# Written order on every engine, weights in 32 pieces, one buffer for each order of v

## The chip, the cores and the metric

The kernel runs on one core of a Trainium2 chip. The metric is the device time of one execution in microseconds (us); lower is better. Every time of a run is a median of several executions, taken on the same chip in the same rounds as the kernel before; readings of a trace are those of one profiled execution. Runs of different rounds stood on different chips: a difference between two such runs is good to some 2 us, and the ratios to before are the safer comparison.

## The reference, cut to what matters

A gated linear attention feeds a two-layer MLP with a quick GELU.

```python
# q, k, v, f_logit: (4, 8, 768, 48) float32
f = 1 / (1 + np.exp(-f_logit))
for t in range(S):
    state = f[:, :, t, :, None] * state + np.einsum('bhd,bhe->bhde', k[:, :, t], v[:, :, t])
    y[:, :, t] = np.einsum('bhd,bhde->bhe', q[:, :, t], state)
x = y.transpose(0, 2, 1, 3).reshape(3072, 384)
h = x @ w_in                                  # (384, 2048)
out = (h * (1 / (1 + np.exp(-1.702 * h)))) @ w_out   # (2048, 384)
```

The weights arrive as 64-bit floats, and the kernel builds 32-bit floats from their two halves.

## The kernel before

The 3,072 tokens are cut into twelve units of 256. For each unit the attention runs as a ladder of steps (six score levels, two transposes of k, the state, the output y). y is copied to yT and moved by DMA into xT, and the MLP matmuls h (on xT and w_in) and o (on g and w_out) follow. The program is written so that MLP matmuls of earlier units stand between the attention steps of the current one, as `fill`.

Only TensorE runs in the order in which the program is written. The framework's scheduler orders all other engines:

```python
ctx.enter_context(tc.manual_schedule(engines={mybir.EngineType.PE}))
```

The transposes by which VectorE brings the loads of f, q and k into place are called turns. A piece of a weight is converted by one ScalarE and six VectorE operations, in a chain:

```python
nc.scalar.activation(a, hi.bitcast(F32), AF.Abs, scale=2.0 ** 112)
ve.tensor_scalar(si, hi, -(1 << 31), -(1 << 31), op0=ALU.bitwise_and, op1=ALU.bitwise_xor)
ve.tensor_scalar(a, a, 2.0 ** 97, None, op0=ALU.max)
ve.scalar_tensor_tensor(si, ai, 3, si, op0=ALU.logical_shift_left, op1=ALU.bitwise_xor)
ve.tensor_scalar(ai, si, -(1 << 23), None, op0=ALU.bitwise_and)
ve.scalar_tensor_tensor(a, lo.bitcast(U32), 2.0 ** -52, a, op0=ALU.mult, op1=ALU.mult)
ve.tensor_tensor(dst, a, s, ALU.add)
```

There are 28 pieces (12 of 512 columns, 16 of 384), converted during units 0 to 2. One buffer holds all orders in which a unit's v is read, and it is loaded after the whole of the last unit:

```python
vl = ld.tile([P, NV, DM], F32, tag="vl", name=f"vl_{n}")      # pool ld has bufs=1
...
            if n + 1 < NALL:
                load(n + 1)          # at the end of a unit's attention
```

One queue, SyncE's, issues every load, every store and the moves from yT to xT.

## Time and profile before

| | before |
|---|---|
| median of 3 (lowest to highest) | 758.95 us (757.6 to 759.25) |
| profiled span | 761.1 us |
| TensorE matmul, busy | 676.3 us (89%) |
| VectorE, busy | 415.4 us (55%) |
| ScalarE, busy | 188.2 us (25%) |
| moved by DMA | 76.4 MB |

The 55% of VectorE is an average of two stages. In the first 200 us it does the conversion besides the attention; after that it is half idle and TensorE binds. The lines that show this stand in the prediction: the row of slices (each digit is the busy tenths of one fortieth of the span), a table of stretches, waits, and a few marks of the timeline.

### The profile page before, as it was taken

The page shows a single profiled execution, that of the slowest core. Times are in us where ns is not written, and L with a number is a line of the kernel's source. Part 1 is how long each engine was busy: PE and PEld are TensorE (multiplying, and loading weights), DVE is VectorE, ACT ScalarE, POOL GpSimd, SP SyncE. Part 2 cuts the span into 40 slices and gives each one's busy share as a digit, 9 for nine tenths or more (in the row PEclk, how much of TensorE's full clock was granted, in tenths as well). Part 3 has the DMA queues.
Part 4 walks back from the last instruction along what each step waited for, and adds up shares of the span by engine and source line. Part 5 has one row for each costly group of instructions (what it writes and reads, how often), then busy time and mean ns, then how long its engine had stood idle before and what let it go on. Part 6 is the DMA issues. An engine that isn't in the chain of part 4 may idle for free.

```text
span 761.1 us, 20034 instructions
## 1 busy us (share of the span) xinstructions
PE 676.3 (89%) x8864; PEld 499.3 (66%) x8864; DVE 415.4 (55%) x679; ACT 188.2 (25%) x365; POOL 38.5 (5%) x80
## 2 busy tenths in 40 slices
PE   0551577879999999999999999999999999999998
PEld 0440355656768768768668678678677687687684
DVE  6779659789565555455455555456445545352020
ACT  1132123132222222222223223222222222132120
POOL 2010002000100100100100100100100001000000
PEclk9955687989999999999999999999999999999999
DMA  9955775857461351441550550550542402100100
GB/s 200 226 122 136 167 158 140 198 151 155 114 134 52 101 136 43 121 119 39 135 134 10 145 135 1 148 130 28 155 98 65 102 12 86 42 13 7 37 0 21
DMA packets 78182, 76.40 MB, mean 100 GB/s; under 512 B 31504, under 2 KB 72976, under 8 KB 78096
## 3 DMA queue, kind: packets, MB, share of 16 engines
q1 hardware_dynamic: 78096, 75.13, 40.6%
q8 instruction: 69, 1.13, 0.7%
q14 instruction: 17, 0.14, 0.1%
HBM read 65.67 MB, written 9.44 MB: 99 GB/s over the span
## 4 chain that ended last, share of the span: by engine, by line
PE 79%; DVE 9%; DMA 6%; SPq 2%; issue 2%; POOL 0%; ACT 0%; DVEq 0%; POOLq 0%; ACTq 0%
PE h L452 32%; PE o L468 31%; PE sc L251 6%; PE y L304 5%; DMA raw<-in_q_dram 2%; DMA bits<-in_moe_w_out_dram 2%; PE sc L378 1%; PE tkn L362 1%; DVE X L290 1%; DMA bits<-in_moe_w_in_dram 1%; PE y L412 1%; DVE a L165 1%; DVE s L162 1%; DMA v_tok<-in_v_dram 1%; DVE A L275 1%
## 5 line engine op out<-in xcount | busy, mean ns | idle before, releaser
L452 PE MATMUL h<-xT,w_in 128*128 128x256 f32 x1152 | 271.8, 388 | 20.2 <-DMA xT<-yT 20.2
L468 PE MATMUL o<-w_out,g 128*128 128x384 f32 x768 | 267.4, 499 | 5.9 <-DVE g L458 5.9
L452 PEld LDWEIGHTS h<-xT,w_in 128*128 128x128 f32 x1152 | 216.7, 193 | 55.4 <-issue 21.5
L468 PEld LDWEIGHTS o<-w_out,g 128*128 128x128 f32 x768 | 144.3, 193 | 101.6 <-DVE g L458 7.7
L458 DVE TENSOR_TENSOR g<-h,sg 128x256 f32<-128x256 f32 x192 | 81.0, 423 | 167.8 <-ACT sg L457 167.8
L457 ACT ACTIVATE sg<-h 128x256 f32<-128x256 f32 x192 | 73.6, 384 | 176.8 <-PE h L452 176.7
L290 DVE TENSOR_TENSOR X<-X,tot 128x1024 f32<-128x1024 f32 x60 | 73.1, 1218 | 37.6 <-PE sc L251 37.6
L294 ACT COPY Kc<-X 128x512 f32<-128x512 f32 x60 | 37.7, 628 | 185.5 <-DVE X L290 185.5
L304 PE MATMUL y<-A,vl 64*48 64x64 f32 (+1 forms) x2688 | 63.4, 237 | 13.8 <-issue 8.4
L304 PEld LDWEIGHTS y<-A,vl 64*48 64x48 f32 x2688 | 52.9, 126 | 18.9 <-issue 12.6
L275 DVE TENSOR_TENSOR A<-sc,masks 128x512 f32<-128x512 f32 (+1 forms) x84 | 62.6, 755 | 0.0
L219 DVE STREAM_TRANSPOSE X<-raw 128x1024 f32<-128x1024 f32 x24 | 49.2, 2051 | 16.0 <-PE sc L251 11.9
L251 PEld LDWEIGHTS sc<-X,Kc 48*64 48x64 f32 x1920 | 35.6, 141 | 24.6 <-issue 13.4
L251 PE MATMUL sc<-X 48*64 48x128 f32 (+1 forms) x768 | 25.4, 274 | 29.6 <-DVE X L219 26.3
L251 PE MATMUL sc<-X,Kc 48*64 48x64 f32 x1920 | 43.3, 230 | 6.3 <-DVE A L275 5.4
L251 PEld LDWEIGHTS sc<-X 48*64 48x64 f32 x768 | 20.3, 149 | 42.0 <-issue 20.2
L234 POOL TENSOR_TENSOR tot<-F 128x512 f32<-128x512 f32 x12 | 12.8, 1065 | 601.7 <-DVE st L393 592.9
L420 ACT COPY yT<-y 48x1024 f32<-48x1024 f32 x24 | 24.2, 1008 | 56.5 <-PE y L412 50.9
L290 DVE TENSOR_TENSOR X<-X,F 128x1024 f32<-128x1024 f32 x12 | 14.7, 1226 | 38.7 <-PE sc L251 38.7
L159 ACT ACTIVATE a<-bits 128x384 f32<-128x384 f32 (+1 forms) x28 | 16.8, 609 | 48.5 <-DVE w_out L166 22.2
L219 DVE STREAM_TRANSPOSE F<-raw 128x1024 f32<-128x1024 f32 x12 | 24.3, 2025 | 4.6 <-DMA raw<-in_f_logit_dram 4.6
L242 DVE TENSOR_TENSOR X<-X,F 128x1024 f32<-128x1024 f32 x12 | 15.4, 1286 | 17.6 <-PE y L412 17.6
(35 smaller groups left out, 274.0 us busy)
## 6 DMA issues: line engine op xcount, KB each, us to landing
vl<-v_tok SPq DMA_DIRECT2D x60, 192.0 KB
bits<-in_moe_w_out_dram SPq DMA_DIRECT2D x16, 384.0 KB
raw<-in_f_logit_dram SPq DMA_DIRECT2D x24, 192.0 KB
bits<-in_moe_w_in_dram SPq DMA_DIRECT2D x12, 384.0 KB
raw<-in_q_dram SPq DMA_DIRECT2D x24, 192.0 KB
raw<-in_k_dram SPq DMA_DIRECT2D x24, 192.0 KB
v_tok<-in_v_dram SPq DMA_DIRECT2D x12, 384.0 KB
vl<-v_tok SPq DMA_DIRECT2D x12, 384.0 KB
```

The lines of the kernel that those rows point to most:

```text
L159: nc.scalar.activation(a, hi.bitcast(F32), AF.Abs, scale=2.0 ** 112)
L219: nc.vector.transpose(out.rearrange("p (a i j) -> p a j i", a=NP, j=R), raw[:, j].rearrange("p a (j d) -> p (a j) d", j=R)[:, :, :32],)
L251: nc.tensor.matmul(out[g * HS:(g + 1) * HS, h, a, :], lhsT=lhs(h, a * U + g * G), rhs=rhs(h, a * U + g * G), start=True, stop=True,)
L275: nc.vector.tensor_tensor(A[:, :, c:c + w].rearrange("p h (x t) -> p h x t", t=64), t["sc"][:, :, c:c + w].rearrange("p h (x t) -> p h x t ...
L290: nc.vector.tensor_tensor(qk, qk, by, ALU.mult)
L294: nc.scalar.copy(Kc.rearrange("p (n m) -> p n m", m=m), X[:, 2].rearrange("p (n two m) -> p n two m", two=2, m=m)[:, :, 0, :],)
L304: nc.tensor.matmul(dst(h, g, a), lhsT=t["vl"][g * 64:(g + 1) * 64, u, (2 * a + h) * D:(2 * a + h + 1) * D], rhs=A(h, g, a), start=(start a ...
L420: nc.scalar.copy(yT[rows(o)].rearrange("p a g t -> p g a t"), py[rows(o)])
L452: nc.tensor.matmul(ph, lhsT=w_in[:, c, ff * P:(ff + 1) * P], rhs=xTs[n][:, c, :], start=(c == 0), stop=(c == NK - 1))
L457: nc.scalar.activation(sg, ph, AF.Sigmoid, scale=1.702)
L458: nc.vector.tensor_tensor(g[ff // FG][:, ff % FG, :], ph, sg, ALU.mult)
L468: nc.tensor.matmul(t["po"], lhsT=g[ff // FG][:, ff % FG, tt * P:(tt + 1) * P], rhs=w_out[:, ff, :], start=(ff == ffs[0]), stop=(ff == ffs[ ...
```

## The change

The intent is to let the program text decide everything: all engines and queues run in the written order, and the text is rearranged to suit. The conversion becomes 32 pieces of 384 columns, dealt out among the steps of the first four units. Each order of v gets its own buffer, loaded as soon as its last reader has been written. Two loads and half of the xT moves go to ScalarE's queue at the start. The core of the diff:

```diff
-    ctx.enter_context(tc.manual_schedule(engines={mybir.EngineType.PE}))
+    ctx.enter_context(tc.manual_schedule())
...
+    def convert(until):
+        until = min(until, len(pieces))
+        while state["done"] < until:
+            while state["begin"] < min(state["done"] + 2, len(pieces)):
+                begin_piece(state["begin"])          # the ScalarE operation
+                state["begin"] += 1
+            n = state["done"]
+            while todo and todo[0][0] == n:
+                todo.pop(0)[1]()                      # the six VectorE operations
+            state["done"] += 1
+            fetch_weights()
...
-        vl = ld.tile([P, NV, DM], F32, tag="vl", name=f"vl_{n}")
+            t = vls[n, u] = ld.tile([P, DM], F32, tag=f"vl{u}", name=f"vl_{n}_{u}")
...
+                queue = nc.scalar if o and n < 2 else nc.sync     # moves yT -> xT
...
-            parts.insert(-1, ("-", units[n + 1][0]))
+            parts.insert(3, ("-", units[n + 1][0]))   # transposes of the next unit's f and q
+            parts.append(("-", units[n + 1][1]))      # its product and the transpose of k
...
         for kind, fn in parts:
+            ready = state["done"]
             fn()
             at += share(kind)
+            convert(first + int(pieces * at / total))
-            while fill and done < columns * at / total:
+            while fill and done < columns * at / total and fill[0][2] <= ready:
...
+    merge(0, fill, 0, steady, 7)
+    merge(1, fill, UNIT // 2 - LAG // 2, steady, 10)
+    merge(2, fill, UNIT - LAG // 2, steady, 11)
+    merge(3, fill, 3 * UNIT // 2, steady, 4)
```

## The prediction

> **What bounds the kernel now.** I read the slices first, then the stretches, then the longest waits of the first 200 us, then the timeline at the places those point to. A unit is 256 tokens of one batch; there are twelve, and the MLP matmuls (h, o) of earlier units fill TensorE between the attention steps of the current one.
>
> Slices, then stretches (length; busy us of PE, PEld, DVE, ACT, POOL; granted clock, DMA share, GB/s):
> ```profile
> PE   0551577879999999999999999999999999999998
> DVE  6779659789565555455455555456445545352020
> PEclk9955687989999999999999999999999999999999
> ...
> 20.00:40.00 20.00, 9.42 (x288) 8.14 (x288) 14.53 (x24) 3.74 (x6) 0.00 (x0) 0.87 0.97 216
> 40.00:60.00 20.00, 10.28 (x280) 8.98 (x280) 14.66 (x20) 5.86 (x8) 3.67 (x6) 0.59 0.40 97
> 60.00:80.00 20.00, 1.99 (x32) 1.61 (x32) 19.93 (x45) 3.80 (x6) 0.00 (x0) 0.50 0.67 161
> 300.00:400.00 100.00, 100.00 (x1390) 72.86 (x1390) 51.30 (x73) 25.14 (x48) 5.64 (x12) 1.00 0.43 106
> ```
> There are two regimes. From about 190 us on TensorE never stops. Before that it has only 119 of 200 us busy (sum of the stretches), much of it at a low clock: the f64 weights are being converted on VectorE, and everything waits for VectorE or DMA. The waits and marks of it:
> ```profile
> PE sc L251 <- DVE X L219: 26.3, 2, 19.9
> PE h L452 <- DMA xT<-yT: 20.2, 1, 20.2
> ...
> 54.28 2.02 ACT L420 COPY yT<-y 48x1024 f32<-48x1024 f32 x2 [4.91 <-PE y L412]
> 73.21 0.72 SPq L423 DMA_DIRECT2D xT<-yT  x1
> 82.77 2.90 PE L452 MATMUL h<-xT,w_in 128*128 128x256 f32 x6 [20.16 <-DMA xT<-yT]
> ...
> 207.46 1.23 DVE L242 TENSOR_TENSOR X<-X,F 128x1024 f32<-128x1024 f32 x1 [1.11 <-PE y L412]
> 373.63 2.04 ACT L420 COPY yT<-y 48x1024 f32<-48x1024 f32 x2 [5.21 <-PE y L412]
> 428.03 2.05 ACT L420 COPY yT<-y 48x1024 f32<-48x1024 f32 x2 [5.18 <-PE y L412]
> 737.03 20.80 PE L468 MATMUL o<-w_out,g 128*128 128x384 f32 x64
> ```
> yT of unit 0 is done at 56.3, but its move to xT is issued at 73.2 because SyncE stands behind weight loads; the first h starts at 82.8. The yT marks of two steady units are 54.4 us apart: a period that is pure TensorE work. The last unit's 96 h take 20.9 us and its 64 o 20.8 us (end of the timeline), so a unit is 41.7 us of MLP and 54.4 - 41.7 = 12.7 us of attention. Total work 12 x 54.4 = 653 us; TensorE ends at 757.8, so **105 us are lost, nearly all before 200 us**. That is all the change can win.
>
> **What the Trainium skill says.** "TensorE: Matmul & The Clock Gate" (Part 1) has VectorE and ScalarE as strict FIFO: an instruction behind a waiting one waits too. The trace agrees (SyncE's queue above shows the same, 17 us). The same part says idle TensorE falls to a half clock: the granted clock is 0.50 at 60-80 and 1.00 from 200. "DMA: Bandwidth & Descriptors" (Issuing engines are not separate DMA queues) says issuing from two engines only saves issue time, as all share 16 DMA engines; the DMA share of 0.97 at 20-40 leaves nothing for a second queue to win there. "Perfetto Trace Analysis" (Identifying the Most-Contended Engine) warns that matmul busy time is no distance to the roofline; I use it only as this program's own work per unit.
>
> **The change part by part.**
> *Conversions.* 28 pieces become 32 of 384 columns. Six VectorE instructions each; start to start in the trace, where nothing lies between dependent ones, 0.27 + 0.39 + 0.59 + 0.39 + 0.59 + 0.47 = 2.7 us:
> ```profile
> 189.55 0.55 DVE L502 TENSOR_TENSOR sum<-sum,o 128x384 f32<-128x384 f32 x1
> 190.02 0.36 DVE L164 TENSOR_SCALAR a<-s 128x384 int32<-128x384 int32 x1
> 190.41 0.56 DVE L165 SCALAR_TENSOR_TENSOR a<-bits,a 128x384 f32<-128x384 uint32 x1
> 191.00 0.56 DVE L166 TENSOR_TENSOR w_out<-a,s 128x384 f32<-128x384 f32 x1
> ```
> Before, the scheduler interleaved two pieces, hiding the gaps (2.2 us for 384 columns, 2.8 for 512): 16 x 2.2 + 12 x 2.8 = 69 us. After, one at a time: 32 x 2.7 = 86 us. The change adds 17 us of VectorE time in the stage where VectorE binds, and removes the waits.
> *Start.* q and v leave on ScalarE's queue and no conversion stands before unit 0's transposes. f now shares bandwidth with q: at the 240 GB/s of the first 10 us (2.0 MB in 8.5 us) both land near 8.4, k near 14.5; F, X, X1, k turns then 2.0 each (1.2 for the product): first score at 16.7 (19.9 before).
> *Unit 0.* Instructions stand in the written order. Scores at the low clock 2.0 us, product 1.2, mask 0.6-1.2, a piece 2.7; the second piece ends near 33.5. Then come two transposes of unit 1's f and q, whose loads stand behind 8.3 MB: at 210 GB/s, about 41-42 us. VectorE waits some 8 us. After that four levels' rest with three pieces, state steps at 59-62, y at 62.3. yT ends 64.4; xT is issued on two queues, landing near 71; two more pieces, X1 and the k turn end at 70.5, score until 72.6, then the first h: **10 us earlier than 82.8**.
> *Unit 1* (10 pieces). VectorE start to start: attention 21.6 (six products 6.8, masks 4.7, three transposes 5.7, X1 1.2, state 3.1), pieces 27, eight g 2.7: 51.3, plus 2.4 where ScalarE issues six xT moves of 0.65 us ahead of a conversion's Abs: ends near 126.5. TensorE has 12.7 + 15 us of work in it: VectorE binds.
> *Unit 2* (11 pieces). 21.6 + 30 less overlap with g and sums: 53 counted step by step, 1.5 for the first score, 2 for steps where TensorE's 5-6.6 us is the longer. Unit 3's first score starts near **183**.
> *What is left then.* Written order has done five blocks of a quarter unit, 52.1 us. Left: 9 x 12.7 + 12 x 41.7 - 52 = 562 us. The same sum for the kernel before, from y of unit 2 at 207.4 with 64.7 us of MLP done, gives 757.4 against 757.8, so the method holds.
> *New losses.* In unit 3 no MLP matmul stands between the state's input and y: VectorE's seven dependent steps, 3 us. In units 4 to 10 the f and q transposes stand in order ahead of the fourth product, in a stretch of h groups; PSUM gives four buffers. From the end of the second h: g done +1.0, transposes +4.9, product +5.95, ScalarE's copy +6.6, third g +7.4; TensorE comes to the seventh h at 0.9 + 1.1 + 0.4 + 3 x 1.3 = +6.3. About 1.2 us a unit, 7 units: 8.4 us.
> Sum: 183 + 562 + 3 + 8.4 + 3.3 (last store, 761.1 - 757.8) = 759.7 profiled; the timed median was 2.1 below the profiled span: **758 us**.
>
> **Rivals.** (1) *The written order starts TensorE early and keeps it busy.* For: the 20 us wait for xT and the scheduler's waits for weights in unit 0 vanish, and v no longer has to wait for the whole unit (TensorE waited 5.3 us for vl). If VectorE flows at the interleaved 2.2 us a piece, 28 pieces up to unit 2 save 14 us: 744. Against: the dependent gaps above. (2) *In-order engines stall each other.* Every h group now waits behind whatever VectorE and ScalarE have before it. If the 1.2 us becomes 3 us a unit and the f and q wait 12 us, it is 775. For: the old order placed these transposes elsewhere (right after the first mask, and among the o matmuls, where no g waits). Against: each step has 4.8 us of MLP to cover it. (3) *DMA stays the bound in the first 60 us.* Smaller rows (1 KB instead of 4 KB for w_in) at a share of 0.97: 20% on 1.6 MB moves all by 2 us. (4) *It is hidden anyway:* TensorE's work is unchanged, so any gain must come before 200 us; before, 65 us of MLP was done by 207; after, 52 us by 183: 13 us less work done, 24 us earlier.
>
> **Range and chances.** The terms pull both ways: earlier unit 3 against less MLP done, then 11 us of new stalls. I take +-8 us for the first three units, +-5 for the stalls, and a little for DMA: 745 to 771. Faster by over 2% (below 743.8) needs rival 1 whole and no stalls: 0.11. Slower by over 2% (above 774.1) needs rival 2: 0.09. Within: 0.80.
>
> **What would show it.** First h near 73; TensorE near full from about 185; VectorE above 90% busy from 70 to 180, with a wait for raw f or q near 35-42; pieces at 2.7 us; steady period 55.6 instead of 54.4, with a wait of TensorE for g or sg once a unit. It is wrong if the steady period is unchanged (then about 750), or if it grows by several us, or if VectorE idles much between 70 and 180.

## The result, and the profile after

The changed kernel is slower: 794.65 us median (793.73 to 796.84, 4 executions) against 759.1 (757.6 to 761.76, 4 executions). The ratio is 1.0469, with a 95% interval of 1.0432 to 1.0505. A ratio here is the mean time of one kernel's runs over that of the other's of the same rounds, so it is not quite the ratio of the medians. The profiled span is 792.5 us at a mean granted clock of 0.958 (before 761.1 at 0.948).

The work grew far less than the time: TensorE is busy 682.5 us (676.3 before), VectorE 434.3 (415.4; the prediction had put 17 us more), ScalarE 185.1 (188.2), and 76.41 MB moved. e1 below converts the same pieces and isn't slower than before, so the added conversion alone does not account for the 36 us; most of them are waiting. The slices of the changed kernel:

```profile
PE   0532563989699999999999999999999999999998
DVE  4587399797756645545546446436445455443020
...
PEclk9996698897899999999999999999999999999999
```

A slice is 19.8 us. From the fourth to the ninth (59 to 178 us) VectorE's row has a 3 and two 7s, where the prediction wanted 9s. The stretches say when (columns: length; busy us of PE, PEld, DVE, ACT, POOL; granted clock, DMA share, GB/s):

```profile
60.00:80.00 20.00, 4.24 (x104) 3.26 (x100) 16.41 (x29) 3.67 (x5) 3.30 (x6) 0.61 0.57 135
80.00:100.00 20.00, 11.52 (x216) 9.00 (x216) 7.99 (x15) 2.25 (x5) 0.00 (x0) 0.71 0.74 171
100.00:120.00 20.00, 13.77 (x261) 9.24 (x263) 19.45 (x34) 6.20 (x13) 0.00 (x0) 0.91 0.74 191
120.00:140.00 20.00, 6.96 (x157) 5.32 (x152) 18.76 (x38) 5.77 (x10) 3.30 (x6) 0.82 0.40 111
140.00:160.00 20.00, 19.35 (x267) 13.71 (x264) 14.88 (x28) 4.59 (x10) 0.00 (x0) 0.84 0.66 161
```

VectorE, the engine that should bind here, works 8 of the 20 us from 80 to 100 and 14.9 of those from 140 to 160.

**The hole at 80 to 91.** The timeline of the changed kernel (start, length, engine, line and operation, output and input, count, then idle time before it and what ended it; "SPq" and "ACTq" are the two queues' issues):

```profile
43.95 2.01 DVE L260 STREAM_TRANSPOSE X<-raw 128x1024 f32<-128x1024 f32 x1 [1.03 <-DMA raw<-in_q_dram]
56.95 12.13 SPq L204 DMA_DIRECT2D raw<-in_q_dram  x4
65.51 0.68 ACTq L469 DMA_DIRECT2D xT<-yT  x1
...
78.92 0.73 SPq L469 DMA_DIRECT2D xT<-yT  x1
...
87.60 3.75 PE L492 MATMUL h<-xT,w_in 128*128 128x256 f32 x8 [12.22 <-DMA xT<-yT]
...
90.95 0.42 DVE L498 TENSOR_TENSOR g<-h,sg 128x256 f32<-128x256 f32 x1 [10.46 <-ACT sg L497]
```

Read it from the bottom. VectorE stands 10.5 us at g, which needs the sigmoid of the first h. That h needs xT. ScalarE's half of the xT moves left at 65.5, but SyncE's half only at 78.9, because four small loads of raw q took SyncE 12 us to issue. The queue's own waits in 40 to 92 us say why (us in total, times, longest):

```profile
SPq L204 <- DMA xT<-yT: 10.5, 1, 10.5
```

A load of raw q has nothing to do with xT. The link is in the build's listing of the two programs (what the framework built from kernel.py, not a trace). SyncE's DMAs and those of ScalarE's queue take their completion semaphores in turn from one set of eight (DMAHW0 to 7), and a DMA waits until the previous user of its semaphore has landed (rows 47 to 49 of SyncE's program, then rows 25 and 26 of ScalarE's):

```
47 L204 DMACopy raw<-in_q_dram 32x4x384 [waits DMAHW0_49,DVE_49]
48 L204 DMACopy raw<-in_q_dram 32x4x352 [waits DMAHW2_49]
49 L204 DMACopy raw<-in_q_dram 32x4x384 [waits DMAHW3_49]

25 L469 DMACopy xT_610<-yT_609 48x3x128 [waits DMAHW2_49,Activation_49]
26 L474 DMACopy xT_610<-yT_609 16x128 [waits DMAHW4_49]
```

In the written order the six xT moves of ScalarE's queue fall between these loads, and one of them owns DMAHW2. The listing says which; the trace says how long. SyncE, at row 48, waits for a move that ScalarE issues 8.6 us after SyncE began these loads (65.51 - 56.95), and its own half of xT stands behind that.

**Unit 2.** It has no such hole, yet it takes long: unit 2's first score is at 139.77, unit 3's at 209.76. VectorE's waits in it are small and in turn, 10.1 us together (4.1 for scores, 3.6 for o, 2.0 for sigmoids, 0.4 for the state's products). VectorE waits for o or a score; o waits for g, which stands behind a whole piece on VectorE:

```profile
139.77 1.99 PE L290 MATMUL sc<-X 48*64 48x128 f32 x32 [11.41 <-DVE X L260]
147.27 2.20 PE L508 MATMUL o<-w_out,g 128*128 128x384 f32 x6 [0.65 <-DVE g L498]
...
141.81 1.23 DVE L329 TENSOR_TENSOR X<-X,F 128x1024 f32<-128x1024 f32 x1 [2.19 <-PE sc L290]
148.22 0.56 DVE L542 TENSOR_TENSOR sum<-sum,o 128x384 f32<-128x384 f32 x1 [1.00 <-PE o L508]
```

**The steady part** went as predicted. The yT marks (starts of the copy of y to yT) stand 55.5 us apart (54.4 before), and TensorE's waits from 250 to 700 us show g, once a unit:

```profile
PE h L492 <- DVE g L498: 5.7, 7, 0.8
```

### The profile page after: what moved, and what is told of

Same layout as the page of the kernel before. It is cut to its first block, busy times and chain, and to the rows that moved or that the text cites. A ratio compares the mean times of both kernels' runs of the same rounds, so it can differ in the third digit from the quotient of the medians.

```text
span 792.5 us, 20135 instructions
## 1 busy us (share of the span) xinstructions
PE 682.5 (86%) x8864; PEld 499.7 (63%) x8864; DVE 434.3 (55%) x709; ACT 185.1 (23%) x369; POOL 37.6 (5%) x80
## 2 busy tenths in 40 slices
DMA packets 82919, 76.41 MB, mean 96 GB/s; under 512 B 31632, under 2 KB 79248, under 8 KB 82832
## 4 chain that ended last, share of the span: by engine, by line
PE 69%; DVE 17%; DMA 7%; issue 4%; ACT 1%; SPq 1%; ACTq 0%; DVEq 0%; POOL 0%; POOLq 0%
PE o L508 30%; PE h L492 25%; PE sc L290 6%; PE y L343 5%; DVE X L260 3%; DVE X L329 3%; DMA vn<-v_tok 3%; DVE s L172 2%; DVE a L175 2%; PE sc L421 1%; DMA v_tok<-in_v_dram 1%; PE tkn L404 1%; DMA raw<-in_q_dram 1%; DVE A L314 1%; PE y L456 1%
## 5 line engine op out<-in xcount | busy, mean ns | idle before, releaser
L508 PE MATMUL o<-w_out,g 128*128 128x384 f32 x768 | 274.6, 506 | 8.3 <-DVE g L498 6.3
L290 PEld LDWEIGHTS sc<-X,Kc 48*64 48x64 f32 x1920 | 36.1, 142 | 40.9 <-ACT Kc L333 24.4
L281 POOL TENSOR_TENSOR tot<-F 128x512 f32<-128x512 f32 x12 | 12.5, 1040 | 634.9 <-DVE st L437 621.4
L329 DVE TENSOR_TENSOR X<-X,F 128x1024 f32<-128x1024 f32 x12 | 14.7, 1226 | 29.4 <-PE sc L290 29.4
L281 POOL TENSOR_TENSOR tot<-tot 128x256 f32<-128x256 f32 (+4 forms) x60 | 24.1, 402 | 4.7
```

The costliest lines, as they stand in the source:

```text
L281: nc.gpsimd.tensor_tensor(tn, t2[:, :, 0], t2[:, :, 1], ALU.mult)
L290: nc.tensor.matmul(out[g * HS:(g + 1) * HS, h, a, :], lhsT=lhs(h, a * U + g * G), rhs=rhs(h, a * U + g * G), start=True, stop=True,)
L329: nc.vector.tensor_tensor(qk, qk, by, ALU.mult)
L508: nc.tensor.matmul(t["po"], lhsT=g[ff // FG][:, ff % FG, tt * P:(tt + 1) * P], rhs=w_out[:, ff, :], start=(ff == ffs[0]), stop=(ff == ffs[ ...
```

## The experiments

Two theories stood at the start. **Theory O**: the order itself costs, since an engine that must follow the text stands at an operation whose operand is late while later ones are ready. **Rival N**: the new text is at fault (smaller pieces, more of them, one at a time, the second queue), whoever orders the engines. (The first expectation calls them P and W.) Seventeen kernels ran, all with correct results. The run of the kernel before beside them had medians of 759.5 to 761.6 us.

| run | edit on which kernel | us | ratio to before, 95% interval |
|---|---|---|---|
| e1_pe_only | change, written order for TensorE alone | 755.86 | 0.9942 [0.9921, 0.9964] |
| e2_one_queue | change, xT all on SyncE | 785.73 | 1.0343 [1.0318, 1.0367] |
| e3_fill_first | change, fill ahead of the pieces | 798.29 | 1.0494 [1.0472, 1.0516] |
| e4_turns_earlier | change, f and q turns a step earlier from unit 3 | 790.38 | 1.0387 [1.0364, 1.0410] |
| e5_before_program_order | before, written order for all | 859.56 | 1.1316 [1.1272, 1.1359] |
| e6_one_queue_pe_only | e1 and e2 | 753.02 | 0.9910 [0.9868, 0.9953] |
| e7_xt_all_on_act | change, xT of units 0, 1 all on ScalarE | 790.30 | 1.0394 [1.0354, 1.0435] |
| e8_fine | change, pieces dealt operation by operation | 789.05 | 1.0406 [1.0359, 1.0453] |
| e9_vectore_free | change, VectorE left to the scheduler | 766.18 | 1.0056 [1.0023, 1.0089] |
| e10_pe_and_vectore | change, written order for TensorE and VectorE | 786.31 | 1.0322 [1.0296, 1.0347] |
| e11_three | e2, e4 and e8 | 776.32 | 1.0190 [1.0157, 1.0223] |
| e12_pairs_pe_only | e6, pieces in pairs | 754.24 | 0.9898 [0.9861, 0.9935] |
| e13_pairs_written | e2, e4, pieces in pairs | 783.27 | 1.0293 [1.0261, 1.0325] |
| e14_keys_first | change, key turn ahead of the last pieces | 785.23 | 1.0315 [1.0286, 1.0344] |
| e15_four | e11 and e14 | 774.12 | 1.0184 [1.0146, 1.0222] |
| e16_late_turns_0 | change, f and q turns of unit 0 later | 788.06 | 1.0358 [1.0322, 1.0394] |
| e17_five | e15 and e16 | 774.84 | 1.0194 [1.0148, 1.0241] |

### Whose order: e1, e5, e9, e10

e1 is the change with one line as it was:

```diff
-    ctx.enter_context(tc.manual_schedule())
+    ctx.enter_context(tc.manual_schedule(engines={mybir.EngineType.PE}))
```

> The changed kernel with program order imposed on TensorE alone, as before; pieces, buffers and queues stay as changed. Theory P (written order on VectorE, ScalarE and the queues is what costs): the steady period returns to 54.4 us and the time falls to about 765 us or below. Rival W (the new places of pieces, fill and loads cost, whoever orders the other engines): it stays at 785 us or above.

It took 755.86 us, 39 less than the change and 0.6% below the kernel before, with the steady marks 54.4 us apart again. Its first h is hardly earlier (84.9 against 87.6), since a late xT ends the wait here too; SyncE stood 13.3 us for a move of xT before it issued a load of v. The first h:

```profile
84.90 3.57 PE L492 MATMUL h<-xT,w_in 128*128 128x256 f32 x8 [25.37 <-DMA xT<-yT]
```

But VectorE has other work meanwhile. The stretches of e1:

```profile
0.00:60.00 60.00, 22.43 (x600) 19.45 (x600) 44.83 (x76) 12.74 (x18) 7.74 (x20) 0.92 0.74 168
60.00:100.00 40.00, 12.68 (x217) 10.24 (x217) 30.24 (x57) 8.70 (x16) 0.00 (x0) 0.61 0.88 206
```

and the same stretches of the change:

```profile
0.00:60.00 60.00, 18.71 (x506) 16.78 (x508) 37.29 (x60) 10.90 (x17) 4.63 (x14) 1.00 0.85 197
60.00:100.00 40.00, 15.76 (x320) 12.26 (x316) 24.41 (x43) 5.92 (x10) 3.30 (x6) 0.66 0.66 153
```

By 100 us VectorE has done 75.1 us of work in e1 (44.83 + 30.24) and 61.7 in the change (37.29 + 24.41). Those 13 us are pieces converted (13 against 9) and block transposes done (8 against 6) while something else was late.

e5 puts the kernel *before* into the written order, with the opposite edit of the same line.

> The kernel before with one thing changed: every engine and queue runs in the written order, nothing else. Theory: the written order by itself costs time, because an in-order engine stands at an operation whose operand is late although later ones are ready (the run with only TensorE in written order was 39 us faster than the change). If the order by itself is to blame, this run is slower than before, by 20 us or more (780 to 850 us), with waits of VectorE and ScalarE in the first units. Rival: it is only the new emission of weights and turns that suits the written order badly; then this run stays within 2% of before (745 to 775 us).

It took 859.56 us, 13% more. So the order costs on either text, and on the old one far more. The two lines and two texts make a square: 759.5 and 859.6 us for the old text (scheduler, written order), 755.9 and 794.7 for the new. The new text is worth 65 us in the written order and 4 under the scheduler; rival N falls. The buffers of v are seemingly a part of those 65 us (no run changes them alone, nor the number of pieces), as the groups of y matmuls suggest (busy us and mean ns, then idle before them and what ended most of it). In e5, with one buffer for all orders of v:

```profile
L304 PE MATMUL y<-A,vl 64*48 64x64 f32 (+1 forms) x2688 | 69.6, 250 | 63.3 <-DMA vl<-v_tok 61.7
```

In the change, with one for each and the loads spread:

```profile
L343 PE MATMUL y<-A,vl 64*48 64x64 f32 (+1 forms) x2688 | 63.3, 238 | 1.4 <-issue 1.4
```

e9 and e10 split the order by engine.

```diff
+    # e9: mybir.EngineType left out for width
+    ctx.enter_context(tc.manual_schedule(engines={PE, Activation, Pool, SP}))
+    # e10
+    ctx.enter_context(tc.manual_schedule(engines={PE, DVE}))
```

> The change with one engine, VectorE, ordered by the scheduler; TensorE, ScalarE, GpSimd and both queues stay in the written order. With only TensorE in the written order the change took 755.9 us, with all engines 794.7. Theory V: the loss is VectorE standing behind a late operand (g 10.5 us in unit 0, sums and products in unit 2); then this run takes 755 to 770 us and unit 3's first score comes near 185 us (209.8 in the change, 182.2 with TensorE alone). Rival Q: the loss is in the order of the queues and of ScalarE (loads and xT held up); then this run stays at 780 us or above, with unit 3's first score above 200 us.

> The counterpart: TensorE and VectorE in the written order, ScalarE, GpSimd and the queues by the scheduler. Theory V (VectorE's written order is the loss): 780 to 800 us, unit 3's first score at 200 to 212 us, and the steady period stays 55.5 us since the wait of TensorE for g is VectorE's. Rival Q: 755 to 770 us.

With VectorE alone left to the scheduler the change takes 766.18, and unit 3's first score comes at 189.2; with VectorE in the written order and ScalarE, GpSimd and the queues free, 786.31, with that score at 205.3. VectorE's order therefore costs 28.5 us (794.7 to 766.2) or 30.5 (755.9 to 786.3), and the order of the rest 8.3 (794.7 to 786.3) or 10.3 (755.9 to 766.2). The two parts nearly add. Theory O holds, three quarters of it on VectorE. The rival of these two runs, the queues and ScalarE, is not refuted but has the smaller part, a quarter.

### The two queues: e2, e7, e6

```diff
 # e2
-                queue = nc.scalar if o and n < 2 else nc.sync
+                queue = nc.sync
 # e7
+                queue = nc.scalar if n < 2 else nc.sync
```

> All xT moves of units 0 and 1 on SyncE's queue, none on ScalarE's. Theory L (the second queue ties the two together: a load of raw q in SyncE's queue waits for a completion slot that a ScalarE xT move holds, and everything behind it in SyncE's queue, the other half of xT included, comes late): first h at about 76 us instead of 87.6, VectorE's 10.5 us wait for g at 80-91 us gone, and about 8 to 12 us less in all, some 783 us. Rival B (loads come late because DMA is full with the smaller rows of w_in): first h at 87 us or later, since 12 issues of 0.65 us now follow one another, and 793 to 797 us.

> The change with all moves of xT of the first two units on ScalarE's queue instead of half. Theory A: what is late is SyncE's half of xT, since it stands in its queue behind loads that wait for a semaphore which the other queue holds; with xT all on the other queue the first h comes at about 73 to 76 us (now 87.6), and the time falls by 5 to 12 us although SyncE's queue is still held up (its loads of raw q and v then come late and cost something in unit 1). Theory B: the queue of SyncE being held is itself the loss, through the late v and masks of unit 1; then the first h is earlier but the time stays within 4 us of 794.7.

With one queue the wait of the raw q loads for xT is gone and the time falls by 9 us to 785.73. With all xT moves on ScalarE's queue SyncE still waits for them, but xT no longer waits for SyncE. The first h, in e2 and then in e7:

```profile
79.48 2.90 PE L492 MATMUL h<-xT,w_in 128*128 128x256 f32 x6 [4.01 <-DMA xT<-yT]
```

```profile
75.66 3.35 PE L492 MATMUL h<-xT,w_in 128*128 128x256 f32 x8
```

In e7 SyncE's queue is held longer:

```profile
SPq L204 <- DMA xT<-yT: 30.3, 5, 14.0
```

Its h comes 12 us earlier, yet its time only 4 us (its interval of the ratio just meets that of the change). Both theories of e7 are half right: the late half of xT is real, and so is the held queue, whose loads come late for the next unit. Taking the tie away (e2) wins more than moving xT out of its reach (e7).

> The change with the written order for TensorE alone, and all moves of xT on SyncE's queue. Theory: the shared completion semaphores of the two queues cost some 9 us in unit 0 in the written order (785.7 against 794.7); here too the first h waited for xT until 84.9 us. If that holds, the first h comes at 70 to 78 us and the time is 745 to 752 us. Rival: with VectorE free to convert meanwhile, the late xT is hidden, since unit 1 and 2 end when VectorE has done its work; then the time stays at 753 to 758 us.

Under the scheduler the same mend brings the first h from 84.9 to 75.8, and the time from 755.9 to 753.0; the intervals of the two ratios overlap, so the gain is not shown. Unit 3's first score comes at 182.2 without and 181.8 with it: where VectorE can do something else meanwhile, the late xT is hidden, as the rival said. e6 is the fastest kernel measured, with e12, 0.9% below before.

### The places in the text: e3, e4, e8, e14, e16

e3 puts `convert(...)` behind the loop that emits the fill.

> In each step the MLP matmuls with their g and sums are written ahead of the conversions of that step instead of behind them; same instructions. Theory C (TensorE's o waits for a g that stands behind a conversion in VectorE's order, then VectorE waits for a score behind that o): unit 2, 73.6 us from y to y, falls by about 10 us, 783 us in all. Rival V (VectorE's sum of work in units 1 and 2 is the bound, order does not matter): 791 to 796 us.

798.29 us, nothing won: unit 1 is not better and unit 3 is later (212.7 against 209.8). The wait moves to other operations: from 20 to 205 us VectorE's waits for scores fall from 12.1 to 8.8 us, and those for sigmoids rise from 12.5 to 18.6.

e8 deals the same operations out one by one between the fill's matmuls:

```diff
             while todo and todo[0][0] == n:
                 todo.pop(0)[1]()
+                yield
...
                 emit()
+                for _ in range(-(-left // steps)):
+                    next(ops, None)
+                    left -= 1
```

> The change with the conversion's operations dealt out one by one behind the matmuls of a step, in place of a whole piece ahead of them; the same work. Theory: in the written order TensorE, VectorE and ScalarE hand the turn to each other (o waits for g behind a whole piece of conversion, 2.7 us, VectorE's next sum waits for o), and that made unit 2 take 73.6 us from y to y. With finer dealing unit 2 takes about 65 us and the time falls by 5 to 10 us. Rival: unit 2 is bound by VectorE's own work or by the transfers of the pieces; then it stays at 72 to 75 us and the time within 3 us of 794.7.

From y of unit 1 to y of unit 2 it takes 66.9 us where the change takes 73.6: the handing to and fro is real. The time is 789.05, 5.6 less, with intervals that overlap a little; the trace's 6.7 us is what I rely on.

```diff
 # e4
-            parts.insert(3, ("-", units[n + 1][0]))
+            parts.insert(3 if n < 3 else 2, ("-", units[n + 1][0]))
 # e16
+            parts.insert(3 if n else 6, ("-", units[n + 1][0]))
```

> From unit 3 on, the next unit's transposes of f and q one step earlier, among o matmuls where no g stands behind them; units 0 to 2 unchanged. Theory S (the wait of TensorE for g, 0.8 us and its echo, once a unit is caused by these transposes): the steady period 55.5 falls to about 54.4, 7 to 8 us in all, 787 us. Rival: they stall TensorE in the new place as well, or the rise of the period has another cause: 793 to 796 us.

> The change with one thing moved: in unit 0 the transposes of unit 1's f and q stand after the levels instead of after the third step, so that their loads have some 12 us more. Theory: the two waits of VectorE (4.8 and 1.0 us at 41 to 44 us) go, y of unit 0 comes at about 58 us instead of 63.4, and unit 3's first score 5 us earlier (204 to 205): 788 to 791 us. Rival: y comes earlier but everything behind it still waits for the transfers of xT and of the pieces: then within 2 us of 794.7.

With e4 the steady marks are 54.4 us apart again and the waits of TensorE for g from 400 to 700 us are gone: 790.38. That is less than the 7 to 8 us expected; in unit 3 TensorE's o now waits 3.9 us for g, where the change has 0.9. With e16 VectorE's waits for raw f and q in unit 0 are gone, unit 1's first score comes at 65.6 instead of 73.4, and the time is 788.06.

e14 has the next unit's key turn and product directly behind the last step, ahead of its pieces:

```diff
-            parts.append(("-", units[n + 1][1]))
+            kind, last_part = parts.pop()
+            parts.append((kind, lambda: (last_part(), units[n + 1][1]())))
```

> The change with one thing moved: the next unit's key turn and its product stand ahead of the last step's conversions instead of behind them. The trace has TensorE wait 11.4 us for that turn before the first score of unit 2 (139.8 us). Theory: that wait is a loss; the first score of unit 2 comes at about 131 us and of unit 3 at 200 us, time 783 to 788 us. Rival: VectorE is busy without a gap in that wait, so the conversions only come later; only its 2.2 us wait for the score after it goes per unit, and the time stays at 789 to 796 us.

785.23 us. TensorE's wait before unit 2's first score falls from 11.4 to 5.7 us, and unit 3's first score comes at 204.7: 5 us of the 9.4. The rival, that the pieces only come later, falls for this part. The edit does more than was meant, though. With the last two steps in one, the loop that emits the fill has one pass fewer, and of the MLP matmuls that the change has ahead of unit 4's first score (264 h and 174 o in the trace) 24 h and 30 o come behind it. (A build of e14 with an empty last step has them back in their place.) The steady marks are 54.4 us apart again, TensorE's waits for g from 400 to 700 us are gone, as with e4, and unit 4's first score waits for its keys instead:

```profile
274.44 1.99 PE L290 MATMUL sc<-X 48*64 48x128 f32 x32 [4.06 <-DVE X L260]
```

### Do the mends add: e11, e15, e17

> Written order for all, with the three mends together: xT on one queue (alone 785.7), transposes one step earlier from unit 3 on (alone 790.4), conversion dealt out finely (alone 789.1), against 794.7. If the three losses are separate they add: 9 + 4 + 6 = 19 us, so 776 us; steady period 54.4, unit 3's first score near 195. Rival: what one mend saves another wait takes, so it stays at 782 to 788 us. In neither case does it come below the kernel before (759).

776.32 us, as the sum of the three gains said.

> The three mends together (776.3) and the key turn ahead as well. Theory (wait for the keys is a loss of 6 to 10 us): 766 to 771 us. Rival (conversions only move): 773 to 778 us. Neither reaches the 755.9 of TensorE alone in the written order.

> The four mends (774.1) and the later transposes of unit 0. If the wait for raw f and q is a separate loss: 767 to 770 us. Rival, the DMA engines (share 1.02 at 20 to 40 us) set the pace of the first 60 us and the waits only move: 772 to 776 us. In neither case is it below 761, since VectorE's order can't follow the arrival of the pieces.

774.12 and 774.84. Alone the fourth mend took 9.4 us and the fifth 6.6; on top of the others they take 2.2 (within the intervals) and nothing. As I read the traces, this has two reasons. First, e4 and e14 take away the same wait: the steady marks are 54.4 us apart with either, so its 1.1 us a unit can be won only once. Second, in e15 unit 3's first score is 6.4 us earlier than in e11 (189.5 against 195.9), but the time from there to the end of the span is 5.7 us longer (582.4 against 576.7). That isn't MLP left over, since both have done 120 h and 78 o matmuls by then; TensorE stands idle longer, 16.4 us against 7.8 (span less busy time), of which 4.1 us before unit 4's first score, as in e14. So e15 ends where its rival put it. In e17 y of unit 0 comes 10 us earlier than in e15 (56.5 against 66.4) but the first h only 1.2 us (81.0 against 82.3), again as the rival had it. That the first three added exactly was therefore no law. With these mends the written order stops at about 774 us here, some 18 us above TensorE alone.

### The gaps in a piece: e12, e13

Both runs also give a and s three buffers in place of two and deal the pieces 8, 10, 10, 4 to the first four units in place of 7, 10, 11, 4.

```diff
+            for x, y in zip(*both):    # the operations of two pieces, alternating
+                x()
+                y()
```

> The fastest so far (TensorE alone in the written order, xT on one queue: 753.0) with the pieces converted in pairs, their operations alternating, so that no operation follows at once the one it depends on. (Three in place of two buffers for a and s; 8, 10, 10 and 4 pieces in place of 7, 10, 11 and 4.) My estimate in the prediction was 2.7 us a piece alone and 2.2 us interleaved; VectorE is 85 per cent busy up to 180 us, and 28 pieces fall before unit 3. If that gap is what binds it, unit 3's first score comes 8 to 14 us earlier (181.8 before) and the time is 740 to 747 us. Rival: the scheduler fills the gaps with other work already, or the start is bound by the transfers; then 750 to 756 us.

> Written order for all; xT on one queue and transposes one step earlier (alone -9 and -4 us: 782 together if they add), and the pieces converted in pairs, operations alternating (8, 10, 10, 4 pieces by unit). Theory: a piece alone takes 2.7 us, in pairs 2.2; 28 pieces fall before unit 3's first score and 14 us of VectorE go: 768 to 773 us, if VectorE's own work is what is left. Rival: in the written order a pair of 4.4 us in one stretch makes o, sums and scores wait longer, so the gain is lost: 778 us or above.

e12 is inconclusive for its question. Its timeline shows the scheduler putting the operations back into single pieces (one piece after another from 68.7 to 79.2 us, 2.7 each), so the 754.24 says nothing of pairs. In e13 the order is kept, and the timeline shows a pair (first, second and last of its six double operations, then what follows):

```profile
126.33 0.61 DVE L170 TENSOR_SCALAR s<-bits 128x384 int32<-128x384 int32 x2
126.86 0.62 DVE L171 TENSOR_SCALAR a<-a 128x384 f32<-128x384 f32 x2
...
129.81 1.02 DVE L176 TENSOR_TENSOR w_in<-a,s 128x384 f32<-128x384 f32 x2
130.74 0.42 DVE L502 TENSOR_TENSOR g<-h,sg 128x256 f32<-128x256 f32 x1
```

Two pieces take 130.74 - 126.33 = 4.41 us, so 2.2 each against 2.7 alone, as the prediction had it. Still the run takes 783.27, about what e2 and e4 should give without it (782, an estimate from their single gains). The saving, 28 pieces of 0.5 us or 14 us before unit 3, turned into waits. From 20 to 205 us VectorE waits 8.1 us for o before its sums (2.0 in e2), 8.0 us for the sigmoid before g (4.1 in e2) and 3.9 us for ScalarE's part of a piece (at most 0.4 in e2): 13 us more. That these waits come from the longer stretches of a pair is my reading; that the saved work did not shorten the run is shown. So in this text it is not the amount of VectorE's work alone that sets the time.

## Why the prediction was wrong

The prediction's sum gave a profiled 759.7 us, and it was 792.5. Held against its own marks (first score of a unit):

| | predicted | change | e1, TensorE alone |
|---|---|---|---|
| unit 1's first score | 70.5 | 73.4 | 57.6 |
| unit 2's | 126.5 | 139.8 | 120.0 |
| unit 3's | 183 | 209.8 | 182.2 |
| from there to the end of the span | 576.7 | 582.7 | 571.7 |

**The start was 3 us late, and unit 0 right again up to y.** The first score was put at 16.7 and came at 19.8 (19.9 before): f was to land at 8.4, at 240 GB/s, but the first 10 us moved 134 GB/s and f could be turned only at 11.9. The wait for raw f and q, put at 35 to 42 us, some 8 us, took the lateness up, since these loads came when predicted: the trace has 4.8 us ending at 40.9 and 1.0 at 43.95. y was put at 62.3, and its copy begins at 63.45. A piece takes 2.7 us alone and 2.2 interleaved.

**"xT is issued on two queues, landing near 71" failed.** The first h came at 87.6, not 73. The step took the second queue as only a saver of issue time. It tied SyncE's queue to ScalarE's through shared completion semaphores (10.5 us), and SyncE's half left at 78.9. e2 prices it at 9 us of time, e9 and e10 put the order of queues and ScalarE together at 8 to 10.

**"VectorE binds" in units 1 and 2, the main failure.** The step summed VectorE's operations from start to start, 56 us for unit 1 and 56.5 for unit 2, with little allowance for VectorE standing (some 4.5 us in unit 1, 3.5 in unit 2). It was 66.4 and 70.0. In unit 1 VectorE stood 14.1 us, 10.5 of them at g. In unit 2 it stood 10.1 us, in the short waits for o, scores and sigmoids; what is left, 59.9 us, is still 7 more than the 53 that the step counted, which had little over 1 us for g and sums, where the trace has 13 g and 5 sums. So the overlap failed in both units, and in unit 2 the work was mis-sized besides. With all engines but TensorE free (e1), unit 3's first score comes at 182.2 us, against 183 predicted, but that agreement is in part luck: e1's unit 1 starts at 57.6, not 70.5, and its units 1 and 2 take 62.4 and 62.2 us. What VectorE's order by itself costs, e9 shows: 28.5 us of time, 20.6 of them by unit 3's first score (189.2 against 209.8).

**The rest of the span was 6 us longer than predicted.** The steady period was right to 0.1 us (55.6 predicted, 55.5 measured), with the wait for g once a unit as foreseen. I have not placed the 6 us exactly. They are not in TensorE's idle time, which is 13.0 us (span less busy time) where the sum had 14.7; TensorE was busy 569.8 us against 562. Part can be the granted clock, 0.76 from 209.8 to 220 us and 0.93 from 280 to 300 (an estimate from these shares: some 4 us). From 200 to 300 us TensorE is busy 90 of 100 us where the prediction had it full from 185, and one wait of 2.0 us of o for a piece of w_out lies there.

**The last step was mis-sized too.** 2.1 us were taken off the profiled sum because the blind median lay below the span. But the timed executions run about 2 us above the span of the same execution (the change: 794.3 timed, 792.5 span). It is the wrong sign, 4 us in all; the profiled execution before (763.1 timed, 761.1 span) was simply slower than its median.

**The rivals.** Rival 2, that in-order engines stall each other, had the right cause and less than half the size (775, 16 us above before, where it was 36). It looked for it in the steady part, "each step has 4.8 us of MLP to cover it"; the stalls came where there is no such cover, in units 0 to 2. Rival 1 (744) fell: flowing at 2.2 us a piece (e13) does not start TensorE earlier. Rival 3 has no run of its own; the first loads came late (11.9 for f), but y came within about 1 us of its mark. Rival 4's premise, that gains must come before 200 us, held for most of the losses as well (26.8 us of 36 by unit 3's first score, against the prediction's mark). "If VectorE idles much between 70 and 180" was among the signs of a wrong prediction, and it is the one that appeared.

**What stays open.** Five mends bring the written order to 774 us, and about 18 us to e1 remain. e9 says most of the whole is VectorE's order, e13 that shorter work alone does not help. Which single waits make the remainder was not settled.

## What to carry to other kernels

A sum of an engine's work is the least time that it needs; if the engine must follow the text, walk through the text with the arrival of each operand, above all where the work of one engine depends on that of two others in turn. When two mends don't add, ask whether both take away the same wait. Before putting all engines in the written order, try it one engine at a time: here TensorE alone was the best, and VectorE's order cost 28 us of 39. After moving DMAs to a second queue, look at the waits of the first queue for names that it has no business with.

## What the Trainium skill lacked or had wrong

- "DMA: Bandwidth & Descriptors" (Issuing engines are not separate DMA queues) says that a second issuing engine only saves issue time. Here the second queue for xT cost 9 us (794.7 against 785.7), since both queues drew their completion semaphores from one set of eight and SyncE stood 10.5 us for a move that ScalarE had yet to issue. No page has this tie, which lies in the program as the framework built it.
- "TensorE: Matmul & The Clock Gate" (Part 1) has VectorE and ScalarE as strict FIFO, and the runs agree. It lacks what that costs a kernel whose text fixes the order: VectorE stood 10.5 us at one g, and left to the scheduler it gave back 28.5 us.
- "VectorE: DVE Perf Modes" (The DRAIN you can't avoid) has the gap behind an operation as one that chaining cannot skip; for operations that nothing holds it points to another section, and the page's rules advise to minimise the count of operations. What the gap costs an operation that must wait for the one before it isn't given there. In these traces a 128x384 operation on two tensors took 0.59 us from start to start before a dependent one and 0.47 in a pair, one on a single tensor 0.39 and 0.27. With the same count, alternating two independent chains took 4.41 us for two pieces where one alone took 2.7, so the gap between dependent operations can be filled. (It did not pay here, for other reasons.)
